# Another order of operations for a fused recurrence and maxout network: the first unit's chain ahead, the gate products in two pairs

## Chip, core and metric

The kernel runs on one core of a Trainium2 chip. The metric is the device time in microseconds (us). The span of a profile is about 1.8 us shorter than the device time of the same execution. Some executions of any kernel are slow as a whole (an execution counts as slow when it took over 1.5% longer than the fastest of the same kernel). Times given are medians of all executions; ratios use fast executions alone, and each kernel is compared with runs of the kernel before on the same chip in the same rounds.

## The reference

A linear recurrence with decay (RWKV style) over 768 steps, for 4 batches and 8 heads of 48, feeds a two-branch network in which the larger branch wins:

```python
for t in range(S):                       # S = 768
    cur = einsum('bhd,bhe->bhde', u[None] * kt, vt)
    y[:, :, t] = einsum('bhd,bhde->bhe', rt, state + cur)
    state = wt[..., None] * state + einsum('bhd,bhe->bhde', kt, vt)
# x = y, rearranged to 3072 tokens x 384
g = np.maximum(x @ w1, x @ w2)           # 384 -> 1024
out = g @ w_out                          # 1024 -> 384, float32
```

The kernel works on 12 units, each 256 steps of one batch. It uses max(a, b) = relu(a - b) + b: the gates come from wd = w1 - w2, and the "+ b" part from one folded weight wc = w2 @ w_out.

## The kernel before

All operations are small functions, and one string gives their order. Each engine executes its own operations in the order in which they stand in that string, so the order is also the order of every queue.

```python
for name in ORDER.split():
    name, _, n = name.partition(".")
    OP[name](int(n or 0))
```

The operations that the argument needs, with the engine of each:

- SyncE (DMA queue): `w k r v` load a unit's inputs (four buffers each), `u` the bonus vector, `w1` the float32 weight w1f, `wt` the transposes of w2 (w2T), `row` writes the last row of the unit's log decay to memory, `WL` reads it back, `out0/1` store.
- GpSimd (POOL): `w2`, `wo` are casting loads; `lp` adds pairs of log decays, `rk`, `rku` multiply r, k and u (the "products of the bonus"), `vb` casts v, `vd` multiplies v by the bonus, `dec`, `S0` carry the state.
- VectorE (DVE): `m z` add up log decays, `rp kp` scale r and k, `dg` sums the bonus, `ev1`, `Sa`, `Tf`, `M0a M0b M1a M1b` mask the scores, `wd` subtracts the weights, `wce` evicts the folded weight.
- ScalarE (ACT): `lw` logarithm, `AO AE iA` exponentials, `ev0`, `S1`, `xT` evicts the recurrence's output, `r0..r3` relu of the gates, `os` evicts the output.
- TensorE (PE): `cs` running sum, `tr` transposes, `kv` state, `yb yi ya` the output y, `sc0 sc1` scores, `g0..g3` gates, `oc oa ob` output product, `wcm` folded weight.

```python
def wd(ko):                                                   # VectorE, two inputs in SBUF
    nc.vector.tensor_sub(wd_sb[:, ko, :], w1f[:, ko, :], w2_sb[:, ko, :])

def gate(n, j):                                               # PE, 6 products; tag "go": two PSUM buffers
    U[n]["g", j] = g = pt_([P, 2, 2, P], F32, "go", 2)
    for f in range(2):
        fo = 2 * j + f
        for ko in range(KO):                                  # all three blocks of wd
            nc.tensor.matmul(g[:, f, :], wd_sb[:, ko, fo * P:(fo + 1) * P], U[n]["xT"][:, :, ko, :], ...)

def relu(n, j):                                               # ScalarE: evicts g, frees its buffer
    nc.scalar.activation(U[n]["gT"][:, 2*j:2*j+2]..., U[n]["g", j]..., AF.Relu)

def z(n):                                                     # VectorE
    nc.vector.tensor_add(MZ[n % 2][:, 1, :, 0:D], ex3(), U[n]["lp"])

def row(n):                                                   # SyncE: reads what z(n + 2) overwrites
    U[n]["row"] = t = drp.tile([1, H * DP], F32, tag="row", name="row")
    nc.sync.dma_start(out=t, in_=MZ[n % 2][P - 1:P, 1].rearrange("b h d -> b (h d)"))
# ... cut: the other operations, each a few lines of this kind
```

SBUF is the on-chip memory of the operands, PSUM the one that PE's products go to.

Of the kernel before, what the change touches and what calls it, by code (L numbers as in the profile page):

```python
# [26 lines left out]
WL.2 sc0.2 oc0.1 oa0.1 rp.3 iA.3 lw.4 lp.4 v.4 w.5 vb.4 k.5 r.5 v.5 w.6 k.6 r.6 ob0.1 oc1.1
os0.1 out0.1 dg.3 vd.3 rk.4 rku.4 M0a.2 M0b.2 ya.2 xT.2 vb.5 kp.3 tr.3 ev1.3 ev0.3 cs.4 m.4 kv.3
Sa.3 S1.3 Tf.3 Wt.1 dec.1 S0.1 oa1.1 ob1.1 os1.1 out1.1 z.4 AO.4 AE.4 yb.3 yi.3 sc1.3 g0.2 g1.2
r0.2 r1.2 g2.2 r2.2 g3.2 r3.2 M1a.3 M1b.3 sc0.3 rp.4 iA.4 lw.5 lp.5 oc0.2 oa0.2 ob0.2 oc1.2  # L30
os0.2 out0.2 dg.4 vd.4 rk.5 rku.5 lw.6 lp.6 M0a.3 M0b.3 ya.3 xT.3 kp.4 tr.4 ev1.4 ev0.4 cs.5
kv.4 Sa.4 S1.4 Tf.4 row.3 WL.3 m.5 oa1.2 ob1.2 os1.2 z.5 AO.5 AE.5 yb.4 yi.4 sc1.4 M1a.4 M1b.4
dg.5 vd.5 rk.6 rku.6 out1.0 g0.3 g1.3 r0.3 r1.3 g2.3 r2.3 g3.3 r3.3 rp.5 iA.5 row.4 WL.4 sc0.4
oc0.3 oa0.3 ob0.3 os0.3 out0.3 v.6 w.7 vb.6 k.7 r.7 M0a.4 M0b.4 ya.4 xT.4 kp.5 tr.5 ev0.5 ev1.5
cs.6 m.6 z.6 kv.5 Sa.5 S1.5 AO.6 AE.6 Tf.5 oc1.3 oa1.3 ob1.3 os1.3 out1.3 Wt.4 dec.4 S0.4 Wt.2
dec.2 S0.2 yb.5 yi.5 sc1.5 M1a.5 M1b.5 g0.4 r0.4 g1.4 r1.4 g2.4 r2.4 g3.4 r3.4 row.5 WL.5 rp.6
iA.6 sc0.5 out1.2 oc0.4 oa0.4 lw.7 lp.7 row.6 ob0.4 os0.4 oc1.4 Wt.3 WL.6 dec.3 S0.3 dg.6 vd.6
rk.7 rku.7 M0a.5 M0b.5 ya.5 xT.5 kp.6 tr.6 ev1.6 ev0.6 cs.7 m.7 kv.6 Sa.6 S1.6 Tf.6 oa1.4 ob1.4
os1.4 z.7 AO.7 AE.7 yb.6 yi.6 sc1.6 M1a.6 M1b.6 g0.5 g1.5 r0.5 r1.5 g2.5 r2.5 g3.5 r3.5 rp.7
iA.7 dg.7 sc0.6 v.7 w.8 k.8 r.8 vb.7 lw.8 lp.8 vd.7 v.8 w.9 vb.8 rk.8 rku.8 oc0.5 oa0.5 ob0.5  # L40
os0.5 oc1.5 out0.5 M0a.6 M0b.6 ya.6 xT.6 kp.7 tr.7 ev0.7 ev1.7 cs.8 m.8 kv.7 Sa.7 S1.7 Tf.7
out0.4 Wt.6 dec.6 S0.6 oa1.5 ob1.5 os1.5 z.8 AO.8 AE.8 yb.7 yi.7 sc1.7 M1a.7 M1b.7 g0.6 g1.6
r0.6 r1.6 g2.6 r2.6 g3.6 r3.6 rp.8 iA.8 out1.4 dg.8 vd.8 sc0.7 lw.9 lp.9 oc0.6 oa0.6 ob0.6 os0.6
M0a.7 M0b.7 ya.7 xT.7 oc1.6 k.9 r.9 rk.9 rku.9 v.9 w.10 k.10 r.10 vb.9 lw.10 lp.10 kp.8 tr.8
ev1.8 ev0.8 cs.9 kv.8 Sa.8 S1.8 oa1.6 ob1.6 os1.6 row.7 WL.7 m.9 z.9 AO.9 AE.9 Wt.5 dec.5 S0.5
out0.6 dg.9 vd.9 rk.10 rku.10 yb.8 yi.8 sc1.8 g0.7 g1.7 r0.7 r1.7 g2.7 r2.7 g3.7 r3.7 M1a.8
M1b.8 sc0.8 rp.9 iA.9 oc0.7 oa0.7 ob0.7 os0.7 oc1.7 M0a.8 M0b.8 ya.8 xT.8 kp.9 tr.9 ev1.9 ev0.9
cs.10 m.10 kv.9 Sa.9 S1.9 oa1.7 ob1.7 os1.7 yb.9 yi.9 sc1.9 z.10 AO.10 AE.10 g0.8 g1.8 r0.8 r1.8
g2.8 r2.8 g3.8 r3.8 M1a.9 M1b.9 sc0.9 oc0.8 oa0.8 ob0.8 oc1.8 rp.10 iA.10 v.10 w.11 vb.10 lw.11
lp.11 k.11 r.11 v.11 dg.10 vd.10 rk.11 rku.11 Wt.7 dec.7 S0.7 out1.5 os0.8 M0a.9 M0b.9 ya.9 xT.9  # L50
# [503 lines left out]
```

## Time and profile before

| | before |
|---|---|
| time, median of 3 runs | 165.98 us (165.58 to 168.37) |
| span of the profiled execution | 163.9 us |
| busy: PE, DVE, ACT, POOL | 83%, 62%, 60%, 58% |
| first gate product g0.0 starts | 40.31 us |
| end of PE's work | 160.42 us |
| one regular unit, oc0 to oc0 | 10.52 us (mean of ten) |

A name with a number behind the point is a unit: g0.3 is the first gate group of unit 3. A line of the profile names the source line (L474 is the gate product, L498 oa and ob, L493 oc, L219 wcm, L239 cs, L327 tr, L395 the scores, L482 the relus; on VectorE L207 wd, L253 z, L269 rp, L310 dg, L273 kp; on GpSimd L235 lp, L294 vb, L304 rku, L315 vd). In e3 and e9 to e12 the lines from wd on stand one further down.

### The profile page before, as it was taken

To read this page: it belongs to the slowest core of one execution; us is meant where nothing else is said; L and a number is where in the kernel's file an instruction comes from. 1 tells how busy PE (TensorE), PEld (TensorE's weight loads), DVE (VectorE), ACT (ScalarE), POOL (GpSimd) and SP (SyncE) were. 2 spreads that over 40 slices of the span, in tenths; PEclk is the share of its full clock that TensorE was granted. 3 is DMA by queue.
4 is the path that set the end of the run, shared out by engine and by line. 5 is a ranking of instruction groups with operands and counts; after the bars stand their busy time and mean duration, and the time that the engine had idled before them with its cause. 6 is when DMAs were issued, how large, how long until landed. Compare 5 with 4: busy or idle time off the path is not lost.

```text
span 163.9 us, 6574 instructions
## 1 busy us (share of the span) xinstructions
PE 136.5 (83%) x2920; PEld 88.9 (54%) x2920; DVE 101.3 (62%) x168; ACT 98.6 (60%) x165; POOL 94.8 (58%) x91
## 2 busy tenths in 40 slices
PE   0041083599999999999999999999999999999991
PEld 0011051266667667666676666756766667666660
DVE  6424489939948669488675795767756848643000
ACT  3206032325867788976777786788857877564641
POOL 7374682557386397798366939879980298200000
PEclk9999999999999999999999999999999999999999
DMA  5999999899934997120692799994962020020203
GB/s 135 248 211 389 337 205 225 157 313 298 277 106 72 309 262 230 56 54 0 170 314 60 177 295 278 254 294 95 307 197 94 8 100 4 4 96 4 98 4 144
DMA packets 62797, 28.19 MB, mean 172 GB/s; under 512 B 57768, under 2 KB 61992, under 8 KB 62768
## 3 DMA queue, kind: packets, MB, share of 16 engines
q1 hardware_dynamic: 61328, 26.19, 59.9%
q0 software_dynamic: 1440, 1.57, 5.9%
q8 instruction: 23, 0.38, 1.0%
q14 instruction: 6, 0.05, 0.1%
HBM read 23.81 MB, written 4.73 MB: 174 GB/s over the span
## 4 chain that ended last, share of the span: by engine, by line
PE 79%; DMA 9%; SPq 4%; POOL 2%; ACT 1%; DVE 1%; issue 1%; ACTq 0%; DVEq 0%; POOLq 0%
PE go L474 21%; PE go L498 20%; PE go L493 8%; DMA w2T_sb<-w_sb 6%; PE ex L239 6%; PE y L457 5%; PE sc L395 5%; PE sc L327 4%; PE go L219 4%; PE y L436 3%; DMA lr<-in_r_dram 3%; PE y L349 3%; SPq L279 2%; PE y L418 2%; SPq L181 1%; POOL rku L299 1%
## 5 line engine op out<-in xcount | busy, mean ns | idle before, releaser
L400 DVE TENSOR_TENSOR M<-sc,mask 128x512 bf16<-128x512 f32 x48 | 31.0, 685 | 14.5 <-PE sc L395 14.5
L474 PE MATMUL go<-xT,wd_sb 128*128 128x256 bf16 x288 | 35.5, 272 | 0.6 <-ACT gT L482 0.3
L498 PE MATMUL go<-wo_sb,gT 128*128 128x384 bf16 x192 | 35.2, 327 | 0.0
L482 ACT ACTIVATE gT<-go 128x512 bf16<-128x512 f32 x48 | 28.5, 597 | 9.6 <-PE go L474 8.0
L474 PEld LDWEIGHTS <-wd_sb 128*128 128x128 bf16 x288 | 27.1, 97 | 7.0 <-issue 2.7
L235 POOL TENSOR_TENSOR lp<-lw 128x384 f32<-128x384 f32 x12 | 12.0, 999 | 24.1 <-ACT lw L230 24.1
L299 POOL TENSOR_TENSOR rku<-lr,lk 128x768 f32<-128x768 f32 x12 | 21.8, 1816 | 6.8 <-DMA lr<-in_r_dram 6.8
L498 PEld LDWEIGHTS <-gT 128*128 128x128 bf16 x192 | 18.0, 98 | 11.6
L304 POOL TENSOR_TENSOR rku<-rku,u_b 128x768 f32<-128x768 f32 x12 | 21.8, 1816 | 1.8 <-DMA u_b<-in_u_dram 1.0
L315 POOL TENSOR_TENSOR vd<-lv,dg 128x768 bf16<-128x768 f32 x12 | 18.7, 1559 | 5.8 <-PE sc L395 3.4
L239 PE MATMUL ex<-lp,triS 128*128 128x384 f32 x24 | 12.4, 603 | 9.7 <-POOL lp L235 9.7
L334 DVE COPY T<-sc 128x1024 bf16<-128x1024 bf16 x12 | 8.3, 692 | 19.0 <-PE sc L327 19.0
L465 ACT CAST xT<-y 128x768 bf16<-128x768 f32 x12 | 12.3, 1027 | 12.7 <-PE y L457 12.6
L503 ACT COPY osb<-go 128x384 f32<-128x384 f32 x24 | 11.5, 479 | 10.8 <-PE go L498 10.6
L334 ACT COPY T<-sc 128x1024 bf16<-128x1024 bf16 x12 | 12.2, 1015 | 7.0 <-PE sc L327 7.0
L493 PE MATMUL go<-wc_sb,xT 128*128 128x384 bf16 x72 | 15.8, 328 | 0.0
L294 POOL CAST vn<-lv 128x768 bf16<-128x768 f32 x12 | 9.9, 825 | 5.7 <-DMA lv<-in_v_dram 5.7
L257 ACT ACTIVATE ex<-mz 128x384 f32<-128x384 f32 x12 | 6.0, 496 | 11.8 <-DVE mz L253 11.7
L395 PE MATMUL sc<-T 48*64 48x128 bf16 x384 | 10.7, 229 | 2.5 <-DVE M L400 2.5
L230 ACT ACTIVATE lw<-lw 128x768 f32<-128x768 f32 x12 | 10.0, 836 | 3.3 <-DMA lw<-in_w_dram 3.3
L269 DVE TENSOR_TENSOR rn<-lr,ex 128x768 bf16<-128x768 f32 x12 | 11.3, 946 | 0.2 <-ACT ex L261 0.2
L310 DVE TENSOR_REDUCE dg<-rku 128x16 f32<-128x768 f32 x12 | 11.3, 945 | 0.0
(51 smaller groups left out, 171.3 us busy)
## 6 DMA issues: line engine op xcount, KB each, us to landing
lw<-in_w_dram SPq DMA_DIRECT2D x12, 384.0 KB, 5.1
lk<-in_k_dram SPq DMA_DIRECT2D x12, 384.0 KB, 5.9
lr<-in_r_dram SPq DMA_DIRECT2D x12, 384.0 KB, 5.5
lv<-in_v_dram SPq DMA_DIRECT2D x12, 384.0 KB, 5.4
out_dram<-osb SPq DMA_DIRECT2D x24, 192.0 KB, 2.2
w1f<-in_moe_w_dram SPq DMA_DIRECT2D x1, 1536.0 KB, 12.8
w_sb<-in_moe_w_dram POOLq DMA_DIRECT2D x1, 768.0 KB, 9.3
wo_sb<-in_moe_w_out_dram POOLq DMA_DIRECT2D x1, 768.0 KB, 9.2
```

The costliest lines, as they stand in the source:

```text
L239: nc.tensor.matmul(EX[:, 0, 0:HD], triS, U[n]["lp"].rearrange("p h d -> p (h d)"))
L299: nc.gpsimd.tensor_mul(t, U[n]["r"], U[n]["k"])
L304: nc.gpsimd.tensor_mul(t, t, u_b.rearrange("p (h d) -> p h d", h=H).unsqueeze(1).to_broadcast([P, 2, H, D]))
L315: nc.gpsimd.tensor_mul(t.rearrange("p i h d -> p h i d"), U[n]["v"], U[n]["dg"].to_broadcast([P, H, 2, D]))
L334: copy(t.rearrange("d j i p q -> d (j i p q)"), U[n]["tr"][b].rearrange("d j i p q -> d (j i p q)"))
L395: nc.tensor.matmul(sc[e][q, p, :], t[d, 1, i, p, :], t[d, 0, :, p, :])
L400: nc.vector.tensor_mul(U[n]["M", i][:, e], U[n]["sc", i][e], mask[:, i].rearrange("s i q -> s (i q)").unsqueeze(1).to_broadcast([P, NP, P]))
L465: nc.scalar.copy(t.rearrange("c b k (q i) -> c (b k) i q", i=2), U[n]["y"][:, :, 0:HD].rearrange("c b (k i q) -> c b k i q", k=KO, i=2))
L474: nc.tensor.matmul(g[:, f, :], wd_sb[:, ko, fo * P:(fo + 1) * P], U[n]["xT"][:, :, ko, :], start=(f == 0 and ko == 0), stop=(f == 1 and ko ...
L482: nc.scalar.activation(U[n]["gT"][:, 2 * j:2 * j + 2].rearrange("p f j t -> p (f j t)"), U[n]["g", j].rearrange("p f j t -> p (f j t)"), A ...
L493: nc.tensor.matmul(t, U[n]["xT"][:, b, ko, :], wc_sb[:, ko, :], start=(ko == 0), stop=False)
L498: nc.tensor.matmul(U[n]["o", b], U[n]["gT"][:, fo, b, :], wo_sb[:, fo, :], start=False, stop=(fo == FO - 1))
```

## The change

Its intent: let PE begin its unbroken run earlier, and arrange the regular units anew. Only the string changes. Both strings hold exactly the same operations. The head of it, with the rest cut:

```diff
-w.0 k.0 r.0 u w2 rk.0 lw.0 lp.0 cs.0 m.0 z.0 rku.0 dg.0 AO.0 AE.0 rp.0 v.0 vb.0 w.1 w1 wd.2 k.1
-lw.1 r.1 iA.0 kp.0 tr.0 ev1.0 ev0.0 kv.0 Sa.0 S1.0 Tf.0 wd.0 lp.1 cs.1 m.1 z.1 row.0 wo vd.0
-yb.0 yi.0 sc1.0 M1a.0 M1b.0 AO.1 AE.1 rp.1 iA.1 rk.1 rku.1 v.1 vb.1 w.2 wt.0 lw.2 lp.2 sc0.0
-M0a.0 WL.0 wcm.0 dg.1 M0b.0 ya.0 xT.0 wd.1 wt.1 wcm.1 wt.2 ...
+w.0 k.0 r.0 u v.0 w.1 lw.0 w2 lp.0 cs.0 m.0 z.0 AO.0 AE.0 rp.0 row.0 iA.0 rk.0 rku.0 dg.0 vb.0
+vd.0 lw.1 lp.1 kp.0 kv.0 Sa.0 S1.0 Tf.0 tr.0 ev1.0 ev0.0 cs.1 m.1 z.1 AO.1 AE.1 yb.0 yi.0 sc0.0
+M0a.0 M0b.0 sc1.0 M1a.0 M1b.0 ya.0 xT.0 w1 wd.1 wd.2 k.1 r.1 v.1 w.2 wo ... wd.0 rp.1 iA.1 g0.0
 ... (both strings go on for some 35 lines)
```

PE's order in a regular unit:

```text
before  tr cs kv oa1 ob1 yb yi sc1 g0 g1 g2 g3 sc0 oc0 oa0 ob0 oc1 ya
after   tr kv g0 g1 yb yi sc1 cs g2 g3 sc0 oc0 oa0 ob0 ya oc1 oa1 ob1
```

More of the change, by code (lines that the diff above doesn't have):

```diff
@@ L17 @@
 ORDER = """
-w.0 k.0 r.0 u w2 rk.0 lw.0 lp.0 cs.0 m.0 z.0 rku.0 dg.0 AO.0 AE.0 rp.0 v.0 vb.0 w.1 w1 wd.2 k.1
-lw.1 r.1 iA.0 kp.0 tr.0 ev1.0 ev0.0 kv.0 Sa.0 S1.0 Tf.0 wd.0 lp.1 cs.1 m.1 z.1 row.0 wo vd.0
-yb.0 yi.0 sc1.0 M1a.0 M1b.0 AO.1 AE.1 rp.1 iA.1 rk.1 rku.1 v.1 vb.1 w.2 wt.0 lw.2 lp.2 sc0.0
-M0a.0 WL.0 wcm.0 dg.1 M0b.0 ya.0 xT.0 wd.1 wt.1 wcm.1 wt.2 vd.1 wce.0 kp.1 tr.1 cs.2 ev1.1 kv.1
-m.2 ev0.1 Sa.1 Tf.1 S1.1 z.2 AO.2 AE.2 wce.1 wcm.2 wce.2 yb.1 yi.1 sc1.1 M1a.1 M1b.1 g0.0 r0.0
-g1.0 r1.0 g2.0 g3.0 r2.0 r3.0 k.2 r.2 rk.2 rku.2 rp.2 iA.2 dg.2 v.2 vb.2 vd.2 w.3 lw.3 lp.3 k.3
@@ L24 @@
-r.3 rk.3 rku.3 v.3 w.4 k.4 r.4 vb.3 sc0.1 oc0.0 oa0.0 ob0.0 os0.0 oc1.0 out0.0 M0a.1 M0b.1 ya.1
-xT.1 Wt.0 dec.0 S0.0 kp.2 tr.2 ev1.2 cs.3 ev0.2 kv.2 Sa.2 S1.2 Tf.2 oa1.0 ob1.0 os1.0 row.1 m.3
-WL.1 z.3 AO.3 AE.3 yb.2 yi.2 sc1.2 M1a.2 M1b.2 g0.1 g1.1 r0.1 r1.1 g2.1 g3.1 r2.1 r3.1 row.2
-WL.2 sc0.2 oc0.1 oa0.1 rp.3 iA.3 lw.4 lp.4 v.4 w.5 vb.4 k.5 r.5 v.5 w.6 k.6 r.6 ob0.1 oc1.1
-os0.1 out0.1 dg.3 vd.3 rk.4 rku.4 M0a.2 M0b.2 ya.2 xT.2 vb.5 kp.3 tr.3 ev1.3 ev0.3 cs.4 m.4 kv.3
-Sa.3 S1.3 Tf.3 Wt.1 dec.1 S0.1 oa1.1 ob1.1 os1.1 out1.1 z.4 AO.4 AE.4 yb.3 yi.3 sc1.3 g0.2 g1.2
@@ L30 @@
-r0.2 r1.2 g2.2 r2.2 g3.2 r3.2 M1a.3 M1b.3 sc0.3 rp.4 iA.4 lw.5 lp.5 oc0.2 oa0.2 ob0.2 oc1.2
-os0.2 out0.2 dg.4 vd.4 rk.5 rku.5 lw.6 lp.6 M0a.3 M0b.3 ya.3 xT.3 kp.4 tr.4 ev1.4 ev0.4 cs.5
-kv.4 Sa.4 S1.4 Tf.4 row.3 WL.3 m.5 oa1.2 ob1.2 os1.2 z.5 AO.5 AE.5 yb.4 yi.4 sc1.4 M1a.4 M1b.4
-dg.5 vd.5 rk.6 rku.6 out1.0 g0.3 g1.3 r0.3 r1.3 g2.3 r2.3 g3.3 r3.3 rp.5 iA.5 row.4 WL.4 sc0.4
-oc0.3 oa0.3 ob0.3 os0.3 out0.3 v.6 w.7 vb.6 k.7 r.7 M0a.4 M0b.4 ya.4 xT.4 kp.5 tr.5 ev0.5 ev1.5
-cs.6 m.6 z.6 kv.5 Sa.5 S1.5 AO.6 AE.6 Tf.5 oc1.3 oa1.3 ob1.3 os1.3 out1.3 Wt.4 dec.4 S0.4 Wt.2
@@ L36 @@
-dec.2 S0.2 yb.5 yi.5 sc1.5 M1a.5 M1b.5 g0.4 r0.4 g1.4 r1.4 g2.4 r2.4 g3.4 r3.4 row.5 WL.5 rp.6
-iA.6 sc0.5 out1.2 oc0.4 oa0.4 lw.7 lp.7 row.6 ob0.4 os0.4 oc1.4 Wt.3 WL.6 dec.3 S0.3 dg.6 vd.6
-rk.7 rku.7 M0a.5 M0b.5 ya.5 xT.5 kp.6 tr.6 ev1.6 ev0.6 cs.7 m.7 kv.6 Sa.6 S1.6 Tf.6 oa1.4 ob1.4
-os1.4 z.7 AO.7 AE.7 yb.6 yi.6 sc1.6 M1a.6 M1b.6 g0.5 g1.5 r0.5 r1.5 g2.5 r2.5 g3.5 r3.5 rp.7
-iA.7 dg.7 sc0.6 v.7 w.8 k.8 r.8 vb.7 lw.8 lp.8 vd.7 v.8 w.9 vb.8 rk.8 rku.8 oc0.5 oa0.5 ob0.5
-os0.5 oc1.5 out0.5 M0a.6 M0b.6 ya.6 xT.6 kp.7 tr.7 ev0.7 ev1.7 cs.8 m.8 kv.7 Sa.7 S1.7 Tf.7
@@ L42 @@
-out0.4 Wt.6 dec.6 S0.6 oa1.5 ob1.5 os1.5 z.8 AO.8 AE.8 yb.7 yi.7 sc1.7 M1a.7 M1b.7 g0.6 g1.6
-r0.6 r1.6 g2.6 r2.6 g3.6 r3.6 rp.8 iA.8 out1.4 dg.8 vd.8 sc0.7 lw.9 lp.9 oc0.6 oa0.6 ob0.6 os0.6
-M0a.7 M0b.7 ya.7 xT.7 oc1.6 k.9 r.9 rk.9 rku.9 v.9 w.10 k.10 r.10 vb.9 lw.10 lp.10 kp.8 tr.8
-ev1.8 ev0.8 cs.9 kv.8 Sa.8 S1.8 oa1.6 ob1.6 os1.6 row.7 WL.7 m.9 z.9 AO.9 AE.9 Wt.5 dec.5 S0.5
-out0.6 dg.9 vd.9 rk.10 rku.10 yb.8 yi.8 sc1.8 g0.7 g1.7 r0.7 r1.7 g2.7 r2.7 g3.7 r3.7 M1a.8
-M1b.8 sc0.8 rp.9 iA.9 oc0.7 oa0.7 ob0.7 os0.7 oc1.7 M0a.8 M0b.8 ya.8 xT.8 kp.9 tr.9 ev1.9 ev0.9
@@ L48 @@
-cs.10 m.10 kv.9 Sa.9 S1.9 oa1.7 ob1.7 os1.7 yb.9 yi.9 sc1.9 z.10 AO.10 AE.10 g0.8 g1.8 r0.8 r1.8
-g2.8 r2.8 g3.8 r3.8 M1a.9 M1b.9 sc0.9 oc0.8 oa0.8 ob0.8 oc1.8 rp.10 iA.10 v.10 w.11 vb.10 lw.11
-lp.11 k.11 r.11 v.11 dg.10 vd.10 rk.11 rku.11 Wt.7 dec.7 S0.7 out1.5 os0.8 M0a.9 M0b.9 ya.9 xT.9
-kp.10 tr.10 ev1.10 ev0.10 cs.11 m.11 kv.10 Sa.10 S1.10 z.11 AO.11 oa1.8 ob1.8 os1.8 yb.10 yi.10
-sc1.10 M1a.10 M1b.10 AE.11 dg.11 vd.11 g0.9 r0.9 g1.9 r1.9 g2.9 r2.9 g3.9 r3.9 rp.11 iA.11
-sc0.10 oc0.9 oa0.9 ob0.9 M0a.10 M0b.10 ya.10 xT.10 out1.7 kp.11 tr.11 ev0.11 ev1.11 out0.7 oc1.9
@@ L54 @@
-vb.11 kv.11 Sa.11 S1.11 oa1.9 ob1.9 out0.8 yb.11 yi.11 sc1.11 M1a.11 M1b.11 out1.6 os0.9 os1.9
-out1.9 g0.10 r0.10 g1.10 r1.10 g2.10 r2.10 g3.10 r3.10 out0.9 sc0.11 oc0.10 oa0.10 ob0.10 os0.10
-oc1.10 out0.10 out1.8 M0a.11 M0b.11 ya.11 xT.11 oa1.10 ob1.10 os1.10 g0.11 r0.11 g1.11 r1.11
-g2.11 r2.11 g3.11 r3.11 oc0.11 oa0.11 ob0.11 os0.11 out0.11 out1.10 oc1.11 oa1.11 ob1.11 os1.11
+w.0 k.0 r.0 u v.0 w.1 lw.0 w2 lp.0 cs.0 m.0 z.0 AO.0 AE.0 rp.0 row.0 iA.0 rk.0 rku.0 dg.0 vb.0
+vd.0 lw.1 lp.1 kp.0 kv.0 Sa.0 S1.0 Tf.0 tr.0 ev1.0 ev0.0 cs.1 m.1 z.1 AO.1 AE.1 yb.0 yi.0 sc0.0
@@ new lines @@
+M0a.0 M0b.0 sc1.0 M1a.0 M1b.0 ya.0 xT.0 w1 wd.1 wd.2 k.1 r.1 v.1 w.2 wo rk.1 rku.1 vb.1 wt.0
+lw.2 lp.2 wd.0 rp.1 iA.1 g0.0 r0.0 dg.1 vd.1 g1.0 r1.0 g2.0 r2.0 kp.1 tr.1 ev1.1 ev0.1 kv.1 Sa.1
+Tf.1 S1.1 cs.2 m.2 g3.0 r3.0 yb.1 yi.1 sc1.1 M1a.1 M1b.1 z.2 AO.2 AE.2 wcm.0 wce.0 sc0.1 M0a.1
+M0b.1 wt.1 wcm.1 wce.1 wt.2 wcm.2 wce.2 k.2 r.2 v.2 w.3 rk.2 rku.2 vb.2 rp.2 iA.2 dg.2 vd.2 lw.3
+lp.3 ya.1 xT.1 oc0.0 oa0.0 ob0.0 os0.0 oc1.0 oa1.0 ob1.0 os1.0 kp.2 tr.2 ev0.2 ev1.2 kv.2 Sa.2
+Tf.2 S1.2 g0.1 r0.1 g1.1 r1.1 k.3 r.3 v.3 rk.3 rku.3 w.4 vb.3 k.4 r.4 v.4 w.5 lw.4 lp.4 yb.2
@@ new lines @@
+yi.2 sc1.2 M1a.2 M1b.2 cs.3 g2.1 g3.1 r2.1 r3.1 row.1 m.3 z.3 AO.3 AE.3 sc0.2 M0a.2 M0b.2 vb.4
+rp.3 iA.3 oc0.1 oa0.1 ob0.1 os0.1 WL.0 Wt.0 dec.0 S0.0 ya.2 xT.2 oc1.1 oa1.1 ob1.1 os1.1 dg.3
+vd.3 rk.4 rku.4 out1.0 kp.3 tr.3 ev1.3 ev0.3 kv.3 Sa.3 S1.3 Tf.3 g0.2 r0.2 g1.2 r1.2 yb.3 yi.3
+sc1.3 M1a.3 M1b.3 k.5 r.5 v.5 w.6 vb.5 cs.4 lw.5 lp.5 g2.2 r2.2 g3.2 r3.2 out0.0 row.2 m.4 z.4
+AO.4 AE.4 WL.1 Wt.1 dec.1 S0.1 sc0.3 M0a.3 M0b.3 lw.6 lp.6 rp.4 iA.4 out1.1 oc0.2 oa0.2 ob0.2
+os0.2 oc1.2 oa1.2 out0.2 row.3 ya.3 xT.3 ob1.2 os1.2 dg.4 vd.4 rk.5 rku.5 kp.4 tr.4 ev0.4 ev1.4
@@ new lines @@
+kv.4 Sa.4 S1.4 Tf.4 g0.3 r0.3 g1.3 r1.3 out0.1 yb.4 yi.4 sc1.4 M1a.4 M1b.4 cs.5 g2.3 r2.3 g3.3
+r3.3 m.5 z.5 AO.5 AE.5 sc0.4 M0a.4 M0b.4 rp.5 iA.5 oc0.3 oa0.3 ob0.3 os0.3 dg.5 vd.5 ya.4 xT.4
+row.4 WL.4 Wt.4 dec.4 WL.2 Wt.2 dec.2 S0.2 oc1.3 oa1.3 ob1.3 os1.3 kp.5 tr.5 ev0.5 kv.5 ev1.5
+Sa.5 S1.5 Tf.5 g0.4 r0.4 g1.4 r1.4 yb.5 yi.5 sc1.5 M1a.5 M1b.5 S0.4 cs.6 m.6 g2.4 r2.4 g3.4 r3.4
+z.6 AO.6 AE.6 sc0.5 M0a.5 M0b.5 k.6 r.6 v.6 vb.6 w.7 rk.6 rku.6 lw.7 lp.7 rp.6 iA.6 out1.3 oc0.4
+oa0.4 ob0.4 os0.4 dg.6 vd.6 ya.5 xT.5 oc1.4 oa1.4 ob1.4 os1.4 kp.6 tr.6 ev0.6 ev1.6 kv.6 Sa.6
@@ new lines @@
+S1.6 Tf.6 g0.5 r0.5 g1.5 r1.5 yb.6 yi.6 sc1.6 M1a.6 M1b.6 row.5 cs.7 m.7 g2.5 r2.5 g3.5 r3.5
+out1.2 z.7 AO.7 AE.7 sc0.6 M0a.6 M0b.6 k.7 r.7 v.7 w.8 vb.7 rk.7 rku.7 lw.8 lp.8 rp.7 iA.7 dg.7
+vd.7 oc0.5 oa0.5 ob0.5 os0.5 WL.3 Wt.3 dec.3 S0.3 ya.6 xT.6 out0.3 oc1.5 oa1.5 ob1.5 os1.5 kp.7
+tr.7 ev0.7 ev1.7 kv.7 Sa.7 S1.7 Tf.7 row.6 g0.6 r0.6 g1.6 r1.6 k.8 r.8 v.8 w.9 rk.8 vb.8 rku.8
+WL.5 Wt.5 dec.5 S0.5 lw.9 lp.9 yb.7 yi.7 sc1.7 M1a.7 M1b.7 cs.8 m.8 out0.4 row.7 g2.6 r2.6 g3.6
+r3.6 out0.5 z.8 AO.8 AE.8 sc0.7 M0a.7 M0b.7 rp.8 iA.8 oc0.6 oa0.6 ob0.6 os0.6 dg.8 vd.8 ya.7
@@ new lines @@
+xT.7 oc1.6 oa1.6 ob1.6 os1.6 out1.5 WL.6 Wt.6 dec.6 S0.6 kp.8 tr.8 kv.8 ev0.8 Sa.8 ev1.8 S1.8
+g0.7 g1.7 r0.7 r1.7 yb.8 yi.8 sc1.8 M1a.8 M1b.8 cs.9 g2.7 r2.7 g3.7 r3.7 m.9 z.9 AO.9 AE.9 sc0.8
+M0a.8 M0b.8 k.9 r.9 v.9 w.10 rk.9 rku.9 lw.10 lp.10 vb.9 rp.9 iA.9 k.10 r.10 v.10 w.11 vb.10
+out1.4 oc0.7 oa0.7 ob0.7 os0.7 out0.7 dg.9 vd.9 ya.8 xT.8 oc1.7 oa1.7 ob1.7 os1.7 kp.9 tr.9
+ev0.9 kv.9 Sa.9 ev1.9 S1.9 g0.8 r0.8 g1.8 r1.8 rk.10 rku.10 out0.6 yb.9 yi.9 sc1.9 M1a.9 M1b.9
+lw.11 lp.11 cs.10 m.10 g2.8 r2.8 g3.8 r3.8 z.10 AO.10 AE.10 sc0.9 M0a.9 M0b.9 rp.10 iA.10 oc0.8
@@ new lines @@
+oa0.8 ob0.8 os0.8 oc1.8 oa1.8 ya.9 xT.9 ob1.8 os1.8 dg.10 vd.10 kp.10 tr.10 kv.10 ev0.10 Sa.10
+ev1.10 S1.10 g0.9 r0.9 g1.9 r1.9 k.11 r.11 v.11 vb.11 rk.11 rku.11 yb.10 yi.10 sc1.10 M1a.10
+M1b.10 cs.11 m.11 g2.9 r2.9 g3.9 r3.9 z.11 AO.11 AE.11 sc0.10 M0a.10 M0b.10 out1.6 rp.11 iA.11
+WL.7 Wt.7 dec.7 S0.7 out1.7 oc0.9 oa0.9 ob0.9 os0.9 ya.10 xT.10 dg.11 vd.11 oc1.9 oa1.9 ob1.9
+os1.9 kp.11 tr.11 ev0.11 kv.11 ev1.11 Sa.11 S1.11 g0.10 r0.10 g1.10 r1.10 out0.8 yb.11 yi.11
+sc1.11 M1a.11 M1b.11 g2.10 r2.10 g3.10 r3.10 sc0.11 M0a.11 M0b.11 out1.8 out0.9 oc0.10 oa0.10
@@ L58 @@
+ob0.10 os0.10 out0.10 ya.11 xT.11 out1.9 oc1.10 oa1.10 ob1.10 os1.10 g0.11 r0.11 g1.11 r1.11
+g2.11 r2.11 g3.11 r3.11 out1.10 oc0.11 oa0.11 ob0.11 os0.11 out0.11 oc1.11 oa1.11 ob1.11 os1.11
 out1.11
```

## The prediction

> **What bounds the kernel now.** I read the page's busy shares first, then the slices, then the chain that ended last, and then the timeline of the first 48 us. Busy shares and slices of the kernel before:
>
> ```profile
> PE 136.5 (83%) x2920; PEld 88.9 (54%) x2920; DVE 101.3 (62%) x168; ACT 98.6 (60%) x165; POOL 94.8 (58%) x91
> ...
> PE   0041083599999999999999999999999999999991
> ```
>
> The reader is to see that TensorE (PE) is far ahead of the other engines, and that it is full from the ninth slice (about 33 us) to the last but one. Only the first eight slices are loose. The table by stretches says it in four rows (columns: stretch, its length, then busy time and instructions of PE, weight loads, DVE, ACT, POOL, clock, DMA share, GB/s):
>
> ```profile
> 0.00:30.33 30.33, 7.26 (x121) 3.91 (x121) 18.16 (x40) 8.61 (x12) 16.45 (x24) 1.00 1.10 243
> 30.33:40.31 9.98, 9.98 (x199) 5.42 (x199) 6.65 (x11) 2.96 (x5) 7.82 (x5) 1.00 1.09 277
> 40.31:160.42 120.11, 119.27 (x2609) 79.58 (x2602) 76.47 (x119) 86.52 (x148) 70.52 (x62) 1.00 0.53 147
> 160.42:163.90 3.48, 0.00 (x0) 0.00 (x0) 0.00 (x0) 0.48 (x1) 0.00 (x0) 1.00 0.36 132
> ```
>
> PE works 7.26 of the first 30.33 us. From there to 160.42 it lacks under 1 us. The time is therefore: when PE's unbroken run starts, plus the work still left, plus a tail of 3.48 us. The chain of waits shows what holds the start:
>
> ```profile
> 9.66 1.66 PE ex L239 x2
> 11.42 0.56 DVE mz L249
> 11.98 0.47 DVE mz L253
> 12.54 0.50 ACT ex L257
> 13.06 0.48 ACT ex L261
> 13.57 0.97 DVE rn L269
> 14.54 3.67 SPq L279
> ...
> 19.66 10.62 DMA w2T_sb<-w_sb
> 30.33 2.74 PE go L219 x8
> ```
>
> The first unit's chain (L239 to L269) reaches SyncE's queue, and then PE waits for the transposed weights w2T until 30.33, because the product wcm.0 (L219, the folded weight) stands in PE's order before ya.0, tr.1 and everything later. The first gate product g0.0 (L474) starts only at 40.31.
>
> **What the Trainium skill says.** "TensorE: Matmul & The Clock Gate", Part 1, says that PE runs at half rate until about 3.4 us of sustained activity, in free-running windows. The trace agrees in kind: eight products of L219 took 2.74 us at 30.33 and 1.41 at 38.12. It warms near 35.4, 5 us into the run, and wcm.0, ya.0 and wcm.1 together lose about 2.3 us. "GPSIMD Engine Reference", section 8, says that GpSimd shares SBUF interfaces with VectorE, with contention when a VectorE instruction has two SBUF inputs. Of the large operations here only wd (L207) has two. Three rows of the timeline, the second and third being its neighbours on the clock:
>
> ```profile
> 18.56 1.45 DVE L207 TENSOR_TENSOR wd_sb<-w1f,w_sb 128x1024 bf16<-128x1024 f32 x1 [4.03 <-DMA w1f<-in_moe_w_dram]
> 23.00 2.65 DVE L207 TENSOR_TENSOR wd_sb<-w1f,w_sb 128x1024 bf16<-128x1024 f32 x1
> ...
> 22.76 1.81 POOL L304 TENSOR_TENSOR rku<-rku,u_b 128x768 f32<-128x768 f32 x1
> ```
>
> GpSimd's rku ran 22.76 to 24.57. The wd at 23.00 waited for its end (1.57 us) and then took 1.08. The one at 18.56 overlapped a GpSimd multiplication ending at 18.92 (0.36 us) and took 1.45, so again 1.09 alone. I estimate 1.09 us for a wd alone, and exclusion rather than a slowdown.
>
> **The change part by part.** It adds and removes no instruction; both orders hold the same operations, and no DMA changes size. What moves:
>
> 1. GpSimd: lp.0 (0.98) goes before rk.0 (1.79). lw.0 ends at 5.05, so lp.0 runs 5.1 to 6.1 instead of 8.62 to 9.60. cs.0, m.0, z.0 come 3.5 us earlier, z.0 ending at 8.9. That is not the whole gain: dg.0 needs rku.0, which needs u_b (10.57), so dg.0 still ends near 13.35.
> 2. VectorE: wd.2 no longer stands ahead of kp.0. kp.0 waited behind it until 19.93 (wd.2 itself waited 4.03 for w1f). Now it follows dg.0: 13.3 to 14.25. That is 6.6 us earlier.
> 3. SyncE: row.0 moves ahead of w1. It has to wait for z.0, so w1 is issued near 9.0 and not at 5.68. In the rates by 2 us, the loads ahead of w1 plus the cast w2 (about 2.95 MB) are only through at about 14 us, so w1f should still land near 18.5 (up to 22 if the late issue costs its full 12.8 us to landing), and k.1, r.1 near 21.
> 4. PE: ya.0 and g0.0, g1.0, g2.0 come ahead of tr.1, and wcm after sc1.1.
>
> Walk of the front with the durations of the rows: v.0 lands 13.44; vb.0 to 14.3, vd.0 to 15.75, lp.1 to 16.75; kv.0, tr.0 14.3 to 16.1; cs.1 (1.65 cold) to 18.4; yb.0, yi.0, sc0.0 (0.44, 0.34, 0.64) to 19.9; m.1, z.1 are done by then; M0a, M0b to 21.35; sc1.0 to 22.05; M1a, M1b to 23.45; ya.0 (1.3) to 24.8; xT.0 to 25.9. Then g0.0 needs all three wd, which now stand on VectorE behind M1b.0. rku.1 holds GpSimd to about 24.5, so they run 24.5 + 3 x 1.09 = 27.8 at best. With GpSimd's lp.2 slipping between them I choose 28.3. g0.0 thus starts at 28.3 instead of 40.31.
>
> Against this 12.0 us stands work that before had done ahead of g0.0 and the new order has not: wcm 3 x 1.41 = 4.23, tr.1 0.57, cs.2 0.84, kv.1 0.38, yb.1 0.28, yi.1 0.24, sc1.1 0.35, together 6.89. And PE is cold at 28.3 after 3.5 us without work, which costs again what it cost before 40.31, 2.3 us. Net: 12.0 - 6.9 - 2.3 = 2.8, and about 0.3 of waits in the last unit (before g2.11) should go. About 3.1 us.
>
> Walking on, I find no wait of PE behind it: kp.1 ends at 31.1 and tr.1 is due at 32.2; w2T and wo are there by about 30 and wcm.0 is due at 36.6; sc0.1 waits about 0.1 for M1b.1. In the regular units (10.5 us each before) tr, kv, g0, g1, yb, yi, sc1, cs, g2, g3, sc0, oc0, oa0, ob0, ya, oc1, oa1, ob1 hold the same work. The tightest place is kp of the next unit: from sc0 VectorE needs M0a, M0b, rp, dg, kp, about 4.0 to 4.25 us, where PE fills 4.45 (oc0 to ob1) before tr. Slack 0.2 to 0.4, so no loss but no room. Sum: span 163.9 - 3.1 = 160.8, device time 165.8 (the profiled execution's) - 3.1 = 162.7; I say 162.5.
>
> **Rivals.**
> - The wd trio takes the place of the transpose as what holds PE. It is in my sum at 28.3, but a GpSimd operation between each two (lp.2 1.0, vb.1 0.8) or a w1f at 22 with later k.1, r.1 puts g0.0 at 30: 164.2. For it: a 2.65 us wd already happened. Against: the trace also shows wd holding GpSimd off (the vd at 31.31 took 2.46 and not 1.48).
> - VectorE or ScalarE becomes the bound in the regular part, with kp's slack gone: 0.2 us in 10 units is 2 us, 164.6. For it: 0.2 us of slack. Against: both engines are at 7.6 and 8.1 of 10.5 us.
> - row.1, now behind two more loads on SyncE, lands late and holds z.3, which overwrites what it reads. Estimate: landing 47.5 to 50 against z.3 near 51. At most 1 us, once: 163.6.
> - The front shrinks more than I say: no GpSimd operation in the trio's way, g0.0 at 26.8: 161.
>
> **Range and chances.** The front is worth plus or minus 1.5, the clock's window plus or minus 0.8 (between 1.7 and 3.4 us lost), and lost slack only adds. Range 160.6 to 164.9. Two per cent under 165.98 is 162.7, in the middle of it; an order that a search preferred speaks a little for the faster side. Faster by over 2%: 0.50; within: 0.46; slower: 0.04.
>
> **What would show it.** Right: kp.0 at 13 to 14; the three wd back to back, 23.5 to 29; g0.0 at 27.5 to 29.5 with products of about 0.21 us for some 5 us; wcm without a wait for w2T; no gap in PE's row after that; a tail of 3.5. Wrong: PE idle between tr and kv of the regular units (kp late), a wd of over 2.5 us, g0.0 after 30, or z.3 waiting for a DMA.

## More of the kernel before

The kernel's tiles in PSUM are `ex` with 2 banks, `sc` 2, `y` 2, `go` 2. The output tiles of `oc`, the gates and `wcm` share the two `go` buffers.

## The result

| | before | after |
|---|---|---|
| time, median of 4 runs | 165.78 us (165.46 to 168.37) | 160.59 us (159.91 to 161.36) |
| ratio to before, 95% interval | | 0.9695 (0.9637 to 0.9752) |
| span of the profiled execution | 163.9 us | 158.9 us |
| g0.0 starts | 40.31 us | 28.47 us |
| end of PE's work | 160.42 us | 155.36 us |
| one regular unit, oc0 to oc0 | 10.52 us | 10.36 us (mean of nine) |

A ratio is the mean time of one kernel's fast runs over that of the other's fast runs of the same rounds, so it is not quite the ratio of the medians. The changed kernel is faster by 3.05%. That is on the lower edge of the predicted range (160.6).

The busy shares and PE's slices of the changed kernel, from its page:

```profile
PE 135.2 (85%) x2920; PEld 90.1 (57%) x2920; DVE 100.4 (63%) x168; ACT 96.9 (61%) x165; POOL 94.7 (60%) x91
...
PE   0402860899999999999899999999999999999991
```

PE is now full from within the eighth slice on. In the fifth slice it works at 0.8, in the sixth at 0.6, and in the seventh hardly at all. The chain of waits (the work that ended last, followed back at each step to what released it) shows what that gap is (start, length, what):

```profile
13.89 0.82 POOL vn L294
14.71 1.44 POOL vd L315
16.15 0.96 POOL lp L235
17.16 1.65 PE ex L239 x2
...
23.49 1.64 DVE wd_sb L207
25.13 0.94 issue
26.06 2.36 DVE wd_sb L207 x2
28.47 4.02 PE go L474 x18
```

The transposed weights are gone from the chain. In their place stands the trio of wd, and g0.0 starts behind it. Three rows of the timeline around it:

```profile
23.25 1.81 POOL L304 TENSOR_TENSOR rku<-rku,u_b 128x768 f32<-128x768 f32 x1
23.40 5.00 DVE L207 TENSOR_TENSOR wd_sb<-w1f,w_sb 128x1024 bf16<-128x1024 f32 x3
27.30 1.80 POOL L294 CAST vn<-lv 128x768 bf16<-128x768 f32 x1 [2.24 <-DMA lv<-in_v_dram]
```

The first wd started on the clock at 23.40, just behind rku.1, and took 2.74 us; the other two took 1.21 each. It could not work until rku.1 ended at 25.06. The cast at 27.30, in turn, took 1.80 instead of 0.82 us, as it met the last wd.

The regular part differs too, which the prediction did not have. In each pair of lines below the chain of waits goes through the gate products of one regular unit: first the kernel before, then the changed one.

```profile
61.40 1.42 PE go L474 x12
62.84 1.47 PE go L474 x12
```

```profile
56.41 1.42 PE go L474 x12
...
59.52 1.31 PE go L474 x12
```

Before, the second half of the gates counts 1.47 us; after, 1.31. The first half takes the same in both. A piece of the chain begins where the piece before it ended, so the two are not quite the same measure. In PE's timeline the 24 products of this unit are one row before, and two rows after:

```profile
61.33 2.98 PE L474 MATMUL go<-xT,wd_sb 128*128 128x256 bf16 x24
```

```profile
56.34 1.48 PE L474 MATMUL go<-xT,wd_sb 128*128 128x256 bf16 x12
...
59.36 1.47 PE L474 MATMUL go<-xT,wd_sb 128*128 128x256 bf16 x12
```

By the starts of the single products in the trace of the kernel before, g1 follows g0 after 0.67 us and g3 follows g2 after 0.66, but g2 follows g1 after 0.85. So before g2 stands a wait of 0.19 us, in each of the units 0 to 10. The difference of the means, 0.16, is smaller because the changed kernel's mean has a unit of 11.01 us in it, with a gap that is told at the end.

The difference of 5.06 us in the end of PE's work divides as follows. The front gives 11.84 (g0.0), less 6.89 of work that before had done by then, less about 2.3 of cold clock (the 18 products take 4.02 instead of about 2.1 us, tr.1 takes 0.91 instead of 0.57): 2.65. The waits of 0.19 us in units 0 to 10 give 2.1. In the last unit oc0 starts 3.00 us after g0, instead of 3.36: 0.35. Single gaps take back about 0.4: they come to 0.7 us in the changed kernel's units 4 and 6 and to 0.3 inside yb.7 in the kernel before. Together 4.7, and 0.3 is left open.

### The profile page after: what moved, and what is told of

It reads as the page before. It is cut to its first block, busy times and chain, and to the rows that moved or that the text cites. A ratio compares the mean times of both kernels' runs of the same rounds, so it can differ in the third digit from the quotient of the medians.

```text
span 158.9 us, 6567 instructions
## 1 busy us (share of the span) xinstructions
PE 135.2 (85%) x2920; PEld 90.1 (57%) x2920; DVE 100.4 (63%) x168; ACT 96.9 (61%) x165; POOL 94.7 (60%) x91
## 4 chain that ended last, share of the span: by engine, by line
PE 82%; DMA 6%; DVE 4%; SPq 2%; POOL 2%; issue 2%; ACT 0%; ACTq 0%; DVEq 0%
PE go L474 22%; PE go L498 20%; PE go L493 9%; PE ex L239 6%; DMA lv<-in_v_dram 6%; PE sc L395 6%; PE y L457 4%; PE sc L327 4%; PE y L436 3%; PE go L219 3%; PE y L349 3%; DVE wd_sb L207 3%; PE y L418 2%; SPq L181 1%; DVE M L400 1%
## 5 line engine op out<-in xcount | busy, mean ns | idle before, releaser
L474 PE MATMUL go<-xT,wd_sb 128*128 128x256 bf16 x288 | 37.6, 282 | 4.8 <-DVE wd_sb L207 4.3
L482 ACT ACTIVATE gT<-go 128x512 bf16<-128x512 f32 x48 | 27.9, 595 | 16.6 <-PE go L474 15.7
L474 PEld LDWEIGHTS <-wd_sb 128*128 128x128 bf16 x288 | 28.0, 100 | 13.3 <-DVE wd_sb L207 4.6
L498 PEld LDWEIGHTS <-gT 128*128 128x128 bf16 x192 | 18.6, 98 | 12.3
L315 POOL TENSOR_TENSOR vd<-lv,dg 128x768 bf16<-128x768 f32 x12 | 17.7, 1476 | 12.0 <-DVE dg L310 11.8
L265 ACT ACTIVATE ex<-mz 128x768 f32<-128x768 f32 x12 | 9.8, 814 | 10.5 <-DVE rn L269 10.5
L294 POOL CAST vn<-lv 128x768 bf16<-128x768 f32 x12 | 10.8, 905 | 3.8 <-DMA lv<-in_v_dram 3.8
```

Of the source, the lines that this page charges most:

```text
L315: nc.gpsimd.tensor_mul(t.rearrange("p i h d -> p h i d"), U[n]["v"], U[n]["dg"].to_broadcast([P, H, 2, D]))
L482: nc.scalar.activation(U[n]["gT"][:, 2 * j:2 * j + 2].rearrange("p f j t -> p (f j t)"), U[n]["g", j].rearrange("p f j t -> p (f j t)"), A ...
L498: nc.tensor.matmul(U[n]["o", b], U[n]["gT"][:, fo, b, :], wo_sb[:, fo, :], start=False, stop=(fo == FO - 1))
```

## The experiments

Twelve kernels were run. Two were wrong on purpose. The others gave correct results.

| run | what | time | ratio to before (95%) |
|---|---|---|---|
| changed kernel | | 160.59 | 0.9695 (0.9637 to 0.9752) |
| e1 | before, r0 and r1 halved | 163.72 | 0.9868 (0.9828 to 0.9909) |
| e2 | after, r0 and r1 halved | 160.25 | 0.9682 (0.9644 to 0.9720) |
| e4 | after, row.0 back behind the loads | 160.02 | 0.9663 (0.9626 to 0.9700) |
| e5 | after, wcm.0 back ahead of ya.0 | 164.63 | 0.9939 (0.9898 to 0.9980) |
| e6 | after, wd.2 back ahead of kp.0 | 162.88 | 0.9813 (0.9771 to 0.9856) |
| e7 | after, rk.0 back ahead of lp.0 | 160.99 | 0.9697 (0.9655 to 0.9739) |
| e8 | after, oa1 ob1 back behind kv | 166.39 | 1.0058 (1.0000 to 1.0117) |
| e3 | after, wd in quarters | 163.86 | 0.9882 (0.9840 to 0.9923) |
| e9 | e3 with lw.2, lp.2 earlier | 158.68 | 0.9583 (0.9544 to 0.9622) |
| e10 | e9 with k.1, r.1 ahead of w1 | 158.71 | 0.9585 (0.9541 to 0.9629) |
| e11 | e10 with wo behind rku.1 | 158.99 | 0.9602 (0.9558 to 0.9646) |
| e12 | e10 with row.1, row.2 early | 158.42 | 0.9534 (0.9483 to 0.9585) |

### Where the regular part's 0.16 us per unit comes from: e1 and e2

The theory: with g0 to g3 together and two `go` buffers, g2 must wait until r0 has evicted g0. A timeline row of the kernel before shows the relus of one unit:

```profile
62.19 1.25 ACT L482 ACTIVATE gT<-go 128x512 bf16<-128x512 f32 x2 [0.23 <-PE go L474]
```

r0 runs from 62.19 to about 62.8 and g2 starts at 62.84. The rival: the array is switched between shapes of product in another sequence. Both kernels were run with r0 and r1 shortened, which leaves PE's work as it is:

```diff
 def relu(n, j):
-    nc.scalar.activation(gT[:, 2*j:2*j+2], g, AF.Relu)
+    nc.scalar.activation(gT[:, 2*j:2*j+FJ(j)], g[:, 0:FJ(j)], AF.Relu)   # FJ = 1 for j < 2, else 2
 # out_g, wrong on purpose: for fo < 4 the even block is read twice
-    gT[:, fo, b, :]
+    gT[:, fo - fo % 2 if fo < 4 else fo, b, :]
```

> The kernel before, with the first two relus of each unit (r0, r1) evicting only half of their tile (wrong result on purpose; the later products read the written half twice, so TensorE's work is the same). Theory A, a wait for a PSUM buffer: in the kernel before, g0 to g3 stand together with two 'go' buffers, and g2 waits about 0.16 us for r0 in each unit (g0 to g3 take about 2.90 us, of which 12 products after another full-array product take 1.31 in the changed kernel). A relu about 0.25 us shorter removes that wait: 0.16 x 11 to 12 units, so about 1.8 us faster, ratio near 0.989, and the group of 24 gate products falls to about 2.75 us. Theory B, the regular part of the changed kernel is faster because of which array shapes follow each other: nothing changes here, ratio 1.000 within 0.003.

> The changed kernel with the same half relus (wrong result on purpose). Theory A: g2 comes over 2 us after g1 here, so r0 is long done, and nothing is to be removed: 0.969 of before as the changed kernel, within 0.003. Theory B: the same. A third theory, that ScalarE limits the changed kernel's regular part: 1 us or more faster than the changed kernel (ratio 0.963 or less).

Measured: the kernel before becomes 1.3% faster, the changed one does not move (0.9682 against 0.9695). In e1's chain of waits the 24 gate products of a unit are one piece:

```profile
61.55 2.73 PE go L474 x24
```

This is 1.42 + 1.31, the changed kernel's sum, against 1.42 + 1.47 in the kernel before. Its row of PE's timeline is 0.19 us shorter than the 2.98 above, and g2 now follows g1 after 0.66 us, as g3 follows g2:

```profile
61.48 2.79 PE L474 MATMUL go<-xT,wd_sb 128*128 128x256 bf16 x24
```

From oc0 to oc0 a unit now takes 10.37 us (mean of ten), against 10.52 before and 10.36 in the changed kernel. So the wait for the PSUM buffer is the whole gain of the regular part, and the array's switches are not. (The traces show that steps at such switches do change: g1 to the next product takes 0.75 us in the changed kernel and 0.66 in e1, cs to the next 0.75 and 0.84. They cancel.) ScalarE's speed is no limit in the changed kernel.

### The condition for taking the gates apart: e8

The changed order puts 1.7 us of other work between g1 and g2 (57.82 to 59.52 in its chain of waits), and it also moved oa1 and ob1 ahead of tr. e8 takes that back in nine units:

```diff
-... ya.n oc1.n-1 oa1.n-1 ob1.n-1 tr.n+1 kv.n+1 g0.n g1.n ...
+... ya.n oc1.n-1 tr.n+1 kv.n+1 oa1.n-1 ob1.n-1 g0.n g1.n ...
```

> The changed kernel with oa1, ob1 (1.3 us of TensorE) back behind tr and kv of the next unit, as before, in nine regular units, while g0, g1 stay apart from g2, g3. My working said that VectorE's way from sc0 to kp takes 4.0 us and that oc0 to ob1 cover it with 0.2 to 0.4 us to spare. Then only 3.3 us cover it here and tr waits 0.7 us in nine units: 6 us slower than the changed kernel, about 166.5 us, ratio 1.005. If kp is not near the limit, no loss: 0.972 or less, and the move of oa1, ob1 is not a condition of the split of the gates.

Measured: 166.39 us, ratio 1.0058, as expected. In e8's chain VectorE now stands between the scores and the transposes of every unit:

```profile
61.13 0.40 PE sc L395 x16
...
62.73 0.94 DVE rn L269
63.67 0.86 DVE dg L310
...
64.55 0.97 DVE kn L273
...
65.56 0.41 PE sc L327 x16
```

The next transposes come at 76.60, so a unit takes 11.04 us: 0.68 more than in the changed kernel, where 0.7 was expected. The move of oa1, ob1 by itself saves no work; it makes room for kp. That holds for VectorE's order as it is here; another order of its operations was not tried.

### The front, part by part: e5, e6, e7, e4

Each of these puts one part of the front back as it was.

e5: the folded weight's first product back ahead of ya.0.

```diff
-sc1.0 ya.0 g0.0 ...        (PE)     wd.0 rp.1 ... z.2 wce.0    (VectorE)
+sc1.0 wcm.0 ya.0 g0.0 ...           wd.0 wce.0 rp.1 ... z.2
```

> The changed kernel with wcm.0 back ahead of ya.0, as before (and wce.0 ahead of rp.1, which its buffer demands). The front theory says that TensorE then waits for w2T until about 30.1, runs wcm.0 cold to 32.9, ya.0 to 34.0, waits for x transposed and starts g0.0 near 35.1, with 127.5 us less 1.9 of work behind 30.1: about 3.7 us slower than the changed kernel, 164.3 us, ratio 0.991. If the transposed weights are not what held the front, under 1 us slower: 0.975 or less.

Measured: 164.63 us, about 2.5% slower than the changed kernel. The wait for the transposes is back in the chain:

```profile
19.68 9.60 DMA w2T_sb<-w_sb
29.33 2.74 PE go L219 x8
```

e6: wd.2 back ahead of kp.0.

```diff
-... rp.0 dg.0 kp.0 ... M1b.0 wd.1 wd.2 wd.0       (VectorE)
+... rp.0 dg.0 wd.2 kp.0 ... M1b.0 wd.1 wd.0
```

> The changed kernel with wd.2 back ahead of kp.0 on VectorE. The front theory: wd.2 waits for w1f until about 19, kp.0 ends near 20.9 and not 14.2, so kv.0, tr.0, cs.1 come 5 us later, M1b.0 ends near 28.4 with two wd left: g0.0 near 30.7, 2.2 us slower than the changed kernel, 162.8 us, ratio 0.982. The rival, that the time of wd behind the first unit's chain is all that counts, so that taking one of the three out of there makes up for the later chain: within 0.5 us, 0.972 or less.

Measured: 162.88 us, 0.9813, where 162.8 was expected. VectorE waits for w1f, and g0.0 comes at 30.87:

```profile
10.76 7.67 DMA w1f<-in_moe_w_dram
...
19.67 0.96 DVE kn L273
...
30.87 4.02 PE go L474 x18
```

The run measures two more things. w1f lands at 18.43, though it was issued 5 us later than in the kernel before, where VectorE's wait for it ended at 18.56; and a wd with nothing in its way takes 1.23 us.

e7: rk.0 back ahead of lp.0 on GpSimd (`w2 rk.0 lp.0 rku.0` in place of `w2 lp.0 rk.0 rku.0`).

> The changed kernel with rk.0 back ahead of lp.0 on GpSimd, one part undone. cs.0, m.0, z.0 come 3.5 us later, rp.0 near 14.5, iA.0 near 15.3, so kp.0 ends near 16.3 and not 14.2, and kv.0, tr.0 delay cs.1 by about 0.9 us (it waits for lp.1 until 17.15 anyway). M1b.0 then ends near 24.4, but rku.1 holds VectorE's wd off until 25.06 in either case. Theory: nothing is lost, within 0.4 us of the changed kernel, ratio 0.967 to 0.971. The rival, that lp.0's place is worth its 3.5 us or a good part of it: 1.5 us or more slower, 0.977 or more.

Measured: 0.9697 against 0.9695. The order that the change's name begins with, the first chain ahead of the bonus product, is worth nothing by itself: kp.0 needs dg.0 in any case, and later the wd trio waits for rku.1.

e4: row.0 back behind w1, k.1 and r.1 on SyncE (`w.1 w1 k.1 r.1 row.0 v.1` in place of `w.1 row.0 w1 k.1 r.1 v.1`).

> The changed kernel with row.0 put back behind w1, k.1 and r.1 on SyncE's queue, as before. My working said that the later issue of w1 costs nothing, as the loads ahead of it fill the DMA engines until about 14 us: within 0.3 us of the changed kernel, ratio 0.968 to 0.972. The rival, that part of the gain comes from the tiny row transfer no longer standing in a full queue ahead of v.1 and w.2: 0.5 us or more slower than the changed kernel, 0.973 or more.

Measured: 0.9663 (0.9626 to 0.9700). The interval holds the changed kernel's 0.9695, so no loss is seen; a small gain of some tenths cannot be told apart. The place of the weights' load among the first loads is not a source of the gain.

### What holds the changed kernel now: e3, e9

Since the trio of wd holds g0.0, wd was computed in four quarters of the columns, so that g0.0 needs a quarter of it:

```diff
-def wd(ko):
-    nc.vector.tensor_sub(wd_sb[:, ko, :], w1f[:, ko, :], w2_sb[:, ko, :])
+def wd(j):
+    f = slice(j * d_ff // 4, (j + 1) * d_ff // 4)
+    nc.vector.tensor_sub(wd_sb[:, :, f], w1f[:, :, f], w2_sb[:, :, f])
 # VectorE: M1b.0 wd.0 wd.1 rp.1 dg.1 kp.1 wd.2 wd.3
 # PE:      g0.0 g1.0 tr.1 kv.1 g2.0 cs.2 g3.0
 # e3, ScalarE: r0.0 iA.1 r1.0 ev0.1 S1.1 r2.0 lw.2;  GpSimd: vb.1 vd.1 lp.2
 # e9, ScalarE: iA.1 r0.0 r1.0 lw.2 ev0.1 S1.1 r2.0;  GpSimd: vb.1 lp.2 vd.1
```

> The changed kernel with wd computed in four column quarters in place of three row blocks, so that g0 needs one quarter (0.8 us) and not all three blocks (3.3 us after GpSimd's rku.1 has let go at 25.1); r0, r1 ahead of the late lw.2 on ScalarE, two quarters behind kp.1, tr.1 and kv.1 ahead of g2. If the trio of wd behind rku.1 is what holds TensorE until 28.47, g0.0 starts near 26 and, with about 0.9 us of waiting for kp.1, 1.6 us are gained: about 159.0 us, ratio 0.960. If something else holds TensorE there as well (x transposed, a load), under 0.5 us are gained: 0.967 or more.

e3 was a miss: 163.86 us, slower than the changed kernel by about 1.9%. g0.0 did start at 25.57. But I had put lw.2 behind r2.0, and the running sum of unit 2 had to wait for it, as e3's timeline shows:

```profile
35.07 1.65 PE L240 MATMUL ex<-lp,triS 128*128 128x384 f32 x2 [3.07 <-POOL lp L236]
```

The wait also kept PE's clock cold: this product takes 1.65 us, and 0.91 warm.

> The quarters of wd again, with lw.2 on ScalarE right behind r1.0 and lp.2 on GpSimd ahead of vd.1. In the last try g0.0 did start at 25.6, but cs.2 then waited 3.07 us for lp.2, since lw.2 stood behind r2.0. Now lp.2 should end near 31.1 and cs.2 start near 31.5: 3 us faster than that try and more by the earlier warm clock, about 160.0 us or less, ratio 0.960 to 0.965. If the time is given back elsewhere in the second unit (vd.1, T1, the cold clock), it ends no better than the changed kernel: 0.968 or more.

e9: 158.68 us, 0.9583 (0.9544 to 0.9622), about 1.2% faster than the changed kernel. g0.0 starts at 25.89 instead of 28.47. So the wd trio did hold the front.

### Going on from there: e10, e11, e12

e10 puts k.1 and r.1 ahead of row.0 and w1 on SyncE, so that rk.1 and rku.1 are over before wd begins.

> The quarters with lw.2 mended, and on SyncE k.1 and r.1 ahead of row.0 and w1. Theory, exclusion between wd and GpSimd's multiplications: r.1 then lands near 17 and not 21.3, rk.1 and rku.1 are through near 21.6, and the first quarter runs at 23.4 and not at 25.0; w1f still lands by 21.5. g0.0 near 24.3 and not 25.9; the second unit's cs.2 waits for lp.2 until about 30.5 (was 32.05). 1.5 us faster than the quarters before it: about 157.2 us, ratio 0.949. If w1f lands after 23.4 or cs.2's wait for lp.2 stays at 32, there is no gain: 0.957 or more.

The front did what was expected: g0.0 started at 24.65 instead of 25.89, and oc0.0 at 38.37 instead of 39.80. The time did not move: 0.9585. A row of VectorE's timeline has the reason:

```profile
49.26 0.56 DVE L254 TENSOR_TENSOR mz<-ex,lp 128x384 f32<-128x384 f32 x1 [2.19 <-DMA row<-mz]
```

z.3 overwrites what the transfer row.1 reads, and row.1 stood behind twelve loads on SyncE and was issued at 46.46. The gain turned into a new wait.

> As the run before, and on GpSimd the load wo behind rku.1 and not ahead of rk.1, so that v.1 and w.2 do not share the DMA engines with it. v.1 should land near 23.5 and not 27.3, w.2 near 25 and not 28.6, so lp.2 no longer holds cs.2: at most 0.5 us faster than the run before, 156.7 us, ratio 0.946. The rivals: the cast vn of v.1 on GpSimd meets the first quarter of wd and holds it 0.8 us, or wo lands after 33.5 and holds wcm.0: then no gain or a loss of up to 1 us, 0.949 or more.

e11: 158.99 us, 0.9602. v.1 landed at 22.9 instead of 24.3, but lw.2 started hardly earlier (28.42 against 28.66), now right behind r1.0, and lp.2 took 1.38 us instead of 1.00 beside two quarters of wd. So cs.2 still waited for lp.2 (0.29 us), and z.3 waited 3.01 us for row.1. No gain.

e12 moves the two rows up:

```diff
-... k.2 r.2 v.2 w.3 k.3 r.3 v.3 w.4 k.4 r.4 v.4 w.5 row.1 WL.0 ... row.2 WL.1
+... k.2 r.2 v.2 w.3 row.1 k.3 r.3 v.3 w.4 row.2 k.4 r.4 v.4 w.5 WL.0 ... WL.1
```

> The run with k.1 and r.1 ahead of w1, with row.1 and row.2 moved up on SyncE's queue, behind w.3 and behind w.4. In that run TensorE was 1.43 us ahead of the quarters alone at oc0.0 (38.37 against 39.80) and gave all of it back near 50, where z.3 waited 2.19 us for the transfer row.1 to read what z.3 overwrites; row.1 stood behind twelve loads and was issued at 46.46. Theory: with the rows early z.3 does not wait, and the 1.4 us stay: about 157.2 us, ratio 0.950. If something else holds TensorE at the same place (r.2's late landing through dg.2 and kp.2, or vd.3), it stays at 158.7, 0.957 or more.

e12: 158.42 us over all runs, 0.9534 (0.9483 to 0.9585) over the fast ones. In its trace row.1 is issued at 35.90, and z.3 no longer waits for a DMA. About half of the expected 1.4 us shows. The profile that could say where the rest is fell in the slow state (granted clock 0.989), with its loads landing later (lw.2 started at 30.24, in e10 at 28.66), so that stays open, and the intervals of e9, e10 and e12 overlap. That e9 and e12 beat the changed kernel is clear, as their intervals lie wholly below its own (0.958 and 0.953 against 0.970); that e12 beats e9 is not shown.

## Why the prediction was right, and where it was not

- **The front: right.** g0.0 at 28.47 for 28.3 in the prediction, the wd trio in place of the transposes, wcm without a wait. e5 and e6 put back one cause each and gave 164.63 and 162.88 us, both within 0.4 us of what the same working expects. The 28.3 was met by luck in part, through errors that cancel: rku.1 ended at 25.06 and not at 24.5; a wd alone takes 1.21 us (1.23 in e6) and not 1.09, which is only what the two wd of the kernel before took after their wait; and no GpSimd operation slipped in between the three wd, for which 0.5 us had been added.
- **The work to be done later and the cold clock: right.** 6.89 us of work moved behind g0.0, and about 2.3 us were lost to the clock, which was warm about 4.8 us after 28.47.
- **lp.0 and the place of w1: right that they do not count.** e7 and e4 show no loss.
- **The regular part: the step that failed.** The prediction says that the new order of a regular unit "hold[s] the same work", and so gives it no gain. The work is the same, but the kernel before had a wait of 0.19 us for a `go` buffer in each unit, hidden inside a row of 24 products. Its worth is about 2 us (e1 gained 1.3%), and e1 and e2 show it. The Trainium skill has the clue, in "Perfetto Trace Analysis", Optimization Strategy: a gap that repeats on the engine that should be full can mean too little PSUM for the next tile. I had looked for gaps in PE's row of the page, where there are none: the wait is inside a group that the page counts as busy.
- **The last unit: right.** The wait before g2.11 fell, and the last unit's gates gave 0.35 us for 0.3.
- **kp's room: right.** e8 took 1.3 us from it and lost 0.68 us a unit.
- **The rivals.** The wd trio as the new bound of the front came true as in the sum. VectorE as the bound did not come true, but is one move away (e8). The wait of z.3 for row.1 did not come in the changed kernel. In e9 it was 0.66 us at no cost to PE (oc0.1 to oc0.2 takes 10.32 us there and in the changed kernel), and in e10, with oc0.0 3.1 us earlier than in the changed kernel, it was 2.19 us and held PE.

One gap of 0.46 us in PE's row near 77.8 of the changed kernel, marked as waiting for nothing, is not explained. Seven of the other runs that start from the changed kernel have one such gap of 0.15 to 0.48 us between 76 and 89 us, and e2, e5, e8 and e11 have none, so the order alone does not make it.

## What to carry to other kernels

When one engine is full from some point on, the time is the start of its unbroken run plus its work, and what counts at the start is only the last wait there: of the four front moves that were put back, two (e4, e7) turned out to be worth nothing alone. Count the waits inside a group of equal instructions as well, by comparing the same group in two places of the order. When a front gets shorter, check the transfers that read what a later operation overwrites; they were on time only by the slack that has just been used up.

## What the Trainium skill lacked or had wrong

- "GPSIMD Engine Reference", section 8, speaks only of contention between GpSimd and VectorE instructions with two SBUF inputs. The runs show one waiting for the other: a wd of 1.21 us took 2.74 when rku.1 had started 0.15 us before it and ended at 25.06, and a cast on GpSimd with a single input took 1.80 us instead of 0.82 beside a wd. This is missing in that section only; elsewhere the skill says that one blocks the other.
- "Perfetto Trace Analysis", Matmuls, says to let groups rotate through PSUM banks. It has no word of how many are enough: two buffers with an eviction of 0.6 us behind a group of 0.65 us of products cost 0.19 us each time, and none when other products of 1.7 us stand between.
- "TensorE: Matmul & The Clock Gate", Part 1, gives about 3.4 us of sustained activity to warm up, in free-running windows. From the start of the unbroken run it took about 5 us here (30.33 to 35.4 before, 28.47 to 33.3 after). Windows that run freely leave room for that; a plain budget of 3.4 us does not.
